# A Fourier filter feeding a gated network: constant third-stage matrix and a reordered first batch

## The chip, the cores and the metric

The kernel runs on one core of one Trainium2 chip. The metric is the device time of one execution in microseconds (us), and a lower time is better. The profile of one execution, taken by the hardware profiler, is read beside it; its span covers the recorded instructions, and the execution's own time is about 2 us longer. The engines are named as the profile names them: PE (matrix products; PEld is its weight load), DVE (vector), ACT (scalar functions), POOL (general purpose), SP (here only an issuer of transfers).

## The reference

```python
def _attn_ref(x, filt_r, filt_i):            # x: 8 x 3136 x 256
    X = np.fft.rfft(x, axis=1)
    F = (filt_r + 1j * filt_i)[None, :, :]
    return np.fft.irfft(X * F, n=x.shape[1], axis=1).astype(np.float32)

def _moe_ref(x, w_in, conv_w, w_out):        # d_ff = 1024
    h = np.maximum(x @ w_in, 0.0)
    ...                                      # conv_out: 3 taps of h along the sequence, a weight per column
    gate = 1.0 / (1.0 + np.exp(-conv_out))
    return (h * gate @ w_out).astype(np.float32)
```

Each batch is filtered in the frequency domain along the sequence, and the filtered sequence goes through the gated network. The weights of the network come as 64-bit floats.

## The kernel before

The sequence of 3136 is split as 112 x 28, and the transform and its inverse are four stages of small matrix products, each done in 14 pieces ("pairs" q, two of 28 columns each). The first stage multiplies by a table `s1` that differs for every column; the second multiplies by one constant matrix `s2`; the filter multiplies the result by the filter's real and imaginary parts (three DVE operations and one POOL add, in `filt`); the third stage multiplies by a table `i1` that differs for every piece; the fourth multiplies by one constant matrix `m2`. The result `y` is kept in SBUF as a rounded part `yh` and a remainder `yl`, since the network's products are made of three products of such parts (`mm3`).

Work stands in two parts of the program.

**The first batch.** No network work can run until batch 0 is through all four stages, so PE has only the transform then. A first loop over q does the first stage into `at`. A second loop over i runs a pipeline: the transposes of pair i (`turn_back`), the second stage of i-1, the third stage of i-4 (`turned_stage`, which puts the pair on the side of the weights and the table on the moving side) into `bt`, and the filter of i-2. After it, four pairs of the first stage of batch 1 (`AHEAD`, by `by_column`) are made and stored to DRAM by transfers that ACT issues. A last loop over q transposes back (`br`), does the fourth stage, and writes `yh` by ACT and `yl` by DVE (`hi_act`, `lo_dve`). Beside it the weights are turned from 64-bit floats into two 32-bit parts: eight chunks, each with seven DVE operations, one POOL add (`to_f32`), two ACT roundings and two POOL subtractions (`split_weights`). A generator hands out these DVE operations a few at a time: `conversion(2)` behind each pair of the first stage, `conversion(1)` behind each i of the second loop, `conversion(2)` behind each pair of the last.

**The stream.** Then a loop over steps m runs the network on units of 510 tokens, eight steps to a unit, with the transform of the next batches in between by a plan: the numbers `at2` and `at4` say at which step of a batch's 48 the second and the fourth stage of a pair stand, and a third stage stands three steps after its second. In this part a third stage is `by_column`, two products of 256 columns with the pair's own table. Units that span two batches are put together in a buffer of their own by `join_tail` and `join_head`, at the steps `tails` and `heads`.

Every engine works through its instructions in the order of the program; the order of transfers on SP is that of the program too. SP's next transfer waits where its buffer is still in use, and all that stands behind it waits as well. The number of buffers is the `bufs` of each tile.

Of the kernel before, what the change touches and what calls it, by code (L numbers as in the profile page):

```python
# [18 lines left out]
N2 = 28  # L19
# [17 lines left out]
def _dft_tables():  # L37
# [7 lines left out]
    n1, n2, c, a = np.arange(N1), np.arange(N2), np.arange(N2), np.arange(N1)  # L45
    s1 = np.zeros((N1, N2, 112))
    m2 = np.zeros((112, N1))
    i1 = np.zeros((2, 2, 28, G, N2, 4))
    for g in range(G):
        for s in range(2):  # L50
            if g == G - 1 and s == 1:
                s1[:, :, 2 * 28 + g] = 1.0
                s1[:, :, 3 * 28 + g] = ((-1.0) ** n1)[:, None]
                m2[2 * 28 + g] = 1.0 / S
                m2[3 * 28 + g] = (-1.0) ** a / S
                i1[0, s, 0, g, :, 2] = 1.0
                i1[1, s, 0, g, :, 2] = (-1.0) ** c
                for j in range(14):
                    if j:
                        w = np.conj(_w(j * c, N2))  # L60
                        i1[0, s, j, g, :, 2] = 2 * w.real
                        i1[1, s, j, g, :, 2] = -2 * w.imag
                    w = np.conj(_w((56 + 112 * j) * c, S))
                    i1[0, s, 14 + j, g, :, 3] = 2 * w.real
                    i1[1, s, 14 + j, g, :, 3] = -2 * w.imag
                continue
# [4 lines left out]
            w = np.conj(_w(k1 * a, N1))  # L71
            m2[2 * s * 28 + g] = 2 * w.real / S
            m2[(2 * s + 1) * 28 + g] = -2 * w.imag / S
            for j in range(28):
                k2, sg = (j, 1) if j < 14 else (41 - j, -1)
                w = np.conj(_w((k1 + 112 * k2) * c, S))
                i1[0, s, j, g, :, 2 * s] = w.real
                i1[1, s, j, g, :, 2 * s] = -sg * w.imag
                i1[0, s, j, g, :, 2 * s + 1] = w.imag
                i1[1, s, j, g, :, 2 * s + 1] = sg * w.real  # L80
# [24 lines left out]
    i1 = i1.reshape(2, 56, G, 112)  # L105
    i1 = np.concatenate([i1[0], np.zeros((8, G, 112)), i1[1]])
    return {"s1": s1, "s2": s2(False), "s2s": s2(True), "one": np.eye(128), "i1": i1, "m2": m2}
# [15 lines left out]
def tile_fft_filter_gated_ffn(  # L123
# [12 lines left out]
    i1: bass.AP,  # L136
    m2: bass.AP,
    out: bass.AP,
# [50 lines left out]
    m2_sb = wc.tile([112, N1], F32, name="m2_sb")  # L189
    s2_sb = wc.tile([112, 120], F32, name="s2_sb")  # L190
    s2s_sb = wc.tile([112, 120], F32, name="s2s_sb")
    one_sb = wc.tile([128, 128], F32, name="one_sb")
# [39 lines left out]

    def second(ps, q, r):
        if q < NP - 1:
            nc.tensor.matmul(ps[0:120], lhsT=s2_sb, rhs=r.rearrange("p j d -> p (j d)"), start=True, stop=True)  # L235
        else:
            for j, m in ((0, s2_sb), (1, s2s_sb)):
                nc.tensor.matmul(ps[0:120, j * D:j * D + D], lhsT=m, rhs=r[:, j], start=True, stop=True)
# [11 lines left out]
    def fourth(ps, br, m=m2_sb):  # L250

        for j in range(2):
            for k in range(KT):
                o = ps[:, (2 * k + j) * N1:(2 * k + j + 1) * N1]
                nc.tensor.matmul(o, lhsT=br[:, j, 128 * k:128 * k + 128], rhs=m, start=True, stop=True)  # L255
# [6 lines left out]
    with (  # L262
# [5 lines left out]
        m2g = sc.tile([112, N1], F32, name="m2g", bufs=1)  # L268
        bt = sc.tile([128, KT, G, 112], F32, name="bt", bufs=1)

        def load_weights(k):
            raws[k] = raw = sc.tile([128, 2, 512], I32, name="raw", bufs=3)
            for part, src in enumerate((w_in, w_out)):
                nc.sync.dma_start(out=raw[:, part], in_=src[:, 512 * k:512 * k + 512])

        def load_conv():
            raws["c"] = raw = sc.tile([128, 2, 512], I32, name="raw", bufs=3)
            nc.sync.dma_start(out=raw[:, 0, 0:6 * NF], in_=conv_w)

        def convert(k):  # L280
# [3 lines left out]
            if k == "c":  # L284
                n = 3 * NF
                yield from to_f32(cw.rearrange("p k f -> p (k f)"), raw[:, 0, 0:2 * n], em[:, 0, 0:n], em[:, 1, 0:n])
            else:
                ws[k] = w = sc.tile([128, 2, 256], F32, name="ws", bufs=4)
                yield from to_f32(w.rearrange("p t n -> p (t n)"), raw.rearrange("p t n -> p (t n)"), em[:, 0], em[:, 1])

        def convert_all():
            for k in range(8):
                yield from convert(k)
                if k + 3 < 8:
                    load_weights(k + 3)
                if k > 0:
                    split_weights(k - 1)
            split_weights(7)

        def split_weights(k):  # L300
            w = ws.pop(k)
            parts = [[t.rearrange("p a b -> p (a b)")[:, 256 * k:256 * k + 256] for t in h] for h in (wi, wo)]
            for part, (wh, wl) in enumerate(parts):
                hi_act(wh, w[:, part])
            for part, (wh, wl) in enumerate(parts):
                lo_pool(wl, w[:, part], wh)
# [29 lines left out]
        with tc.tile_pool(name="sq", bufs=2) as sq:  # L336
            at = sq.tile([128, KT, N2, 112], F32, name="at", bufs=1)

            def table(kind, c):
                k, src, n = {"1": (112, s1, 7), "3": (120, i1, 3)}[kind]  # L340
# [395 lines left out]
```

## Time and profile before

| | before |
|---|---|
| median of 3 runs | 1586.04 us (1582.65 to 1586.32) |
| the profiled execution's own time | 1583.21 us |
| its span | 1581.2 us |
| PE busy | 1532.2 us, 97% of the span |
| DVE, ACT, POOL busy | 75%, 73%, 52% |
| last `yl` of batch 0 begins | 118.06 us |

The table gives shares of the whole span. The first 119 us and the rest have different limits, so the prediction reads them apart, by stretches of time.

### The profile page before, as it was taken

Reading aid. Unit: us, or ns where it says so; the run is one execution under the profiler, and the core shown is the slowest. Engines: PE = TensorE matmul, PEld = TensorE weight load, DVE = VectorE, ACT = ScalarE, POOL = GpSimd, SP = SyncE. Lnnn points to the kernel's source line nnn. Section 1 sums busy time; section 2 is a strip of 40 time slices with the busy share of each in tenths; the row PEclk is TensorE's granted clock in tenths of the full one; section 3 lists DMA queues with packets and bytes.
Section 4 is the critical chain, followed back from the end, with each engine's and each line's share of the span. In section 5 each row is a group of like instructions: output and inputs, shape, how many; then the busy total and the mean of one; then the engine's idle time right before and its main releaser. Section 6 shows DMA issues by size and latency. Waiting matters only on the chain.

```text
span 1581.2 us, 26837 instructions
## 1 busy us (share of the span) xinstructions
PE 1532.2 (97%) x9384; PEld 1334.5 (84%) x9384; DVE 1180.3 (75%) x1810; ACT 1150.4 (73%) x1989; POOL 821.7 (52%) x703
## 2 busy tenths in 40 slices
PE   6879999999999999999999999999999999999999
PEld 5777789878898889988898878987899878989998
DVE  5856876677767877777766787777866887777776
ACT  3367668866687668866688667876678666888886
POOL 2623455544575455744556454754457445664444
PEclk9989999999999999999999999999999999999999
DMA  9808764366634674277543766246742553300000
GB/s 271 261 24 246 226 192 140 119 204 178 186 88 143 201 218 125 74 209 210 155 139 107 212 179 184 85 148 198 211 135 63 179 155 106 96 14 28 27 28 30
DMA packets 160592, 229.16 MB, mean 145 GB/s; under 512 B 16546, under 2 KB 109578, under 8 KB 160458
## 3 DMA queue, kind: packets, MB, share of 16 engines
q1 hardware_dynamic: 159497, 226.53, 48.0%
q8 instruction: 75, 1.23, 0.3%
q10 hardware_dynamic: 960, 0.92, 0.2%
q14 instruction: 60, 0.48, 0.1%
HBM read 156.74 MB, written 70.65 MB: 144 GB/s over the span
## 4 chain that ended last, share of the span: by engine, by line
PE 87%; DMA 3%; issue 3%; ACT 2%; DVE 2%; POOL 1%; SPq 0%; ACTq 0%; POOLq 0%; DVEq 0%
PE ps_h L175 11%; PE ps_h L176 11%; PE ps_h L177 11%; PE po L514 11%; PE po L515 11%; PE po L516 11%; PE ps_t L231 10%; PE ps_t L255 6%; PE ps_t L235 5%; DMA rows<-in_x 1%; DMA f<-in_filt 1%; POOL g L150 1%; DMA tab<-in_i 1%; ACT y L144 0%; ACT br L327 0%
## 5 line engine op out<-in xcount | busy, mean ns | idle before, releaser
L482 DVE SCALAR_TENSOR_TENSOR t<-ps_h,cw,t 128x510 f32<-128x510 f32 (+1 forms) x800 | 588.3, 736 | 308.2 <-ACT t L478 305.0
L150 POOL TENSOR_TENSOR g<-t,g 128x510 fp32r<-128x510 f32 (+1 forms) x400 | 505.8, 1273 | 219.5 <-ACT g L144 203.9
L514 PE MATMUL po<-wo,g 128*128 128x256 f32 (+1 forms) x1576 | 439.3, 279 | 0.2 <-DVE ot L527 0.2
L515 PE MATMUL po<-wo,g 128*128 128x256 f32 (+1 forms) x1576 | 438.3, 278 | 0.0
L516 PE MATMUL po<-wo,g 128*128 128x256 f32 (+1 forms) x1576 | 438.0, 278 | 0.0
L473 ACT ACTIVATE ps_h<-ps_h 128x512 f32<-128x512 f32 (+1 forms) x400 | 234.7, 587 | 242.2 <-PE ps_h L177 240.7
L478 ACT ACTIVATE t<-ps_h,cw 128x510 f32<-128x510 f32 (+1 forms) x400 | 272.7, 682 | 103.4 <-POOL g L150 71.3
L247 POOL TENSOR_TENSOR z<-z,v 120x512 f32<-120x512 f32 x112 | 148.0, 1322 | 383.4 <-DVE v L246 314.6
L175 PE MATMUL ps_h<-y,wi 128*128 128x512 f32 (+1 forms) x688 | 325.3, 473 | 0.0
L514 PEld LDWEIGHTS po<-wo,g 128*128 128x128 f32 (+1 forms) x1576 | 296.6, 188 | 17.8 <-ACT t L478 0.6
L515 PEld LDWEIGHTS po<-wo,g 128*128 128x128 f32 (+1 forms) x1576 | 296.2, 188 | 16.6
L516 PEld LDWEIGHTS po<-wo,g 128*128 128x128 f32 (+1 forms) x1576 | 296.4, 188 | 0.6 <-POOL g L150 0.5
L176 PE MATMUL ps_h<-y,wi 128*128 128x512 f32 (+1 forms) x688 | 269.4, 392 | 0.2 <-DVE y L147 0.2
L488 DVE TENSOR_TENSOR t<-ps_h,t 128x510 f32<-128x510 f32 (+1 forms) x400 | 268.4, 671 | 0.9 <-ACT t L485 0.8
L177 PE MATMUL ps_h<-y,wi 128*128 128x512 f32 (+1 forms) x688 | 269.0, 391 | 0.0
L485 ACT ACTIVATE t<-t 128x510 f32<-128x510 f32 (+1 forms) x400 | 245.2, 613 | 1.8 <-DVE t L482 1.7
L144 ACT ACTIVATE g<-t 128x510 fp32r<-128x510 f32 (+1 forms) x400 | 245.1, 613 | 0.2 <-DVE t L488 0.2
L150 POOL TENSOR_TENSOR y<-z,y 128x448 fp32r<-128x448 f32 x98 | 138.7, 1425 | 97.4 <-ACT y L144 92.9
L175 PEld LDWEIGHTS ps_h<-y,wi 128*128 128x128 f32 x688 | 129.9, 189 | 35.9 <-issue 16.6
L176 PEld LDWEIGHTS ps_h<-y,wi 128*128 128x128 f32 x688 | 130.4, 190 | 34.4 <-issue 16.7
L177 PEld LDWEIGHTS ps_h<-y,wi 128*128 128x128 f32 x688 | 129.6, 188 | 29.8
L226 ACT ACTIVATE st<-ps_t 112x512 f32<-112x512 f32 x192 | 113.2, 591 | 10.9 <-PE ps_t L231 10.9
(81 smaller groups left out, 1657.9 us busy)
## 6 DMA issues: line engine op xcount, KB each, us to landing
filt<-in_filt SPq DMA_DIRECT2D x98, 512.0 KB
tin<-a_dram SPq DMA_DIRECT2D x98, 224.0 KB
b_dram<-st SPq DMA_DIRECT2D x98, 224.0 KB
tin<-b_dram SPq DMA_DIRECT2D x98, 224.0 KB
tin<-in_x SPq DMA_DIRECT2D x94, 224.0 KB
a_dram<-st SPq DMA_DIRECT2D x94, 224.0 KB
out<-ot SPq DMA_DIRECT2D x45, 256.0 KB
tab<-in_i SPq DMA_DIRECT2D x98, 105.0 KB
```

The lines of the kernel that those rows point to most:

```text
L144: nc.scalar.activation(dst, src, AF.Copy)
L150: nc.gpsimd.tensor_tensor(out=dst, in0=src, in1=hi.bitcast(F32), op=ALU.subtract)
L175: nc.tensor.matmul(ps, lhsT=wh, rhs=rh, start=start, stop=False, **kw)
L176: nc.tensor.matmul(ps, lhsT=wh, rhs=rl, start=False, stop=False, **kw)
L177: nc.tensor.matmul(ps, lhsT=wl, rhs=rh, start=False, stop=stop, **kw)
L478: nc.scalar.activation(t, hs[u, f][:, 1:n + 1], AF.Copy, scale=cw[:, 1, f:f + 1])
L482: nc.vector.scalar_tensor_tensor(out=t, in0=h[:, k:place(u)[2] + k], scalar=cw[:, k, f:f + 1], in1=t, op0=ALU.mult, op1=ALU.add)
L485: nc.scalar.activation(ts[u, f], ts[u, f], AF.Sigmoid)
L488: nc.vector.tensor_mul(ts[u, f], hs.pop((u, f))[:, 1:place(u)[2] + 1], ts[u, f])
L514: nc.tensor.matmul(o, lhsT=gh[:, c:c + n], rhs=wo[0][:, f], start=first, stop=False, skip_group_check=True)
L515: nc.tensor.matmul(o, lhsT=gh[:, c:c + n], rhs=wo[1][:, f], start=False, stop=False, skip_group_check=True)
L516: nc.tensor.matmul(o, lhsT=gl[:, c:c + n], rhs=wo[0][:, f], start=False, stop=last, skip_group_check=True)
```

## The change

The third stage's twiddle factors are moved to the fourth stage's tables. With that the third stage's matrix is one constant (`s3`, and `s3s` for the one special column), and the fourth stage has a table for each of its 28 columns (`m2`, and `m2g` with its rows in another order for the first batch). In the stream the third stage becomes one product of 512 columns, and the tables that are loaded are those of the first and the fourth stage. In the first batch the constant matrix is copied once by POOL into `by_r`, in the order in which the third stage reads it; before, each table was read there with a step of four elements.

The weight conversion in the first batch moves: three DVE operations behind each pair of the first stage from q = 2 on, none in the second loop up to i = 14, three behind each of its last three turns, two behind each pair of the last loop. POOL makes the rounding that ACT made. Four chunks of weights are loaded among the first stage's data instead of two, the other four late in the second loop. The filters have five buffers instead of three. The four pairs of batch 1 stand inside the second loop's last turns. In the stream `at4` and `heads` move by one step or two.

```diff
+    def s3(special):
+        m = np.zeros((2, 2, 28, N2, 4))
...
+                w = np.conj(_w(k2 * c, N2))
...
-            w = np.conj(_w(k1 * a, N1))
+            w = np.conj(_w(k1 * n, S))
             m2[2 * s * 28 + g] = 2 * w.real / S
...
+    def by_row(o, q, r, m, ms):
+        if q < NP - 1:
+            nc.tensor.matmul(o, lhsT=m, rhs=r.rearrange("p j d -> p (j d)"), start=True, stop=True)
+        else:
+            for j, t in ((0, m), (1, ms)):
+                nc.tensor.matmul(o[:, j * D:j * D + D], lhsT=t, rhs=r[:, j], start=True, stop=True)
...
+    def third(ps, q, z):
+        by_row(ps[0:112], q, z, s3_sb, s3s_sb)
...
-                nc.tensor.matmul(o, lhsT=br[:, j, 128 * k:128 * k + 128], rhs=m, start=True, stop=True)
+                nc.tensor.matmul(o, lhsT=br[:, j, 128 * k:128 * k + 128], rhs=tab[:, j], start=True, stop=True)
...
             for part, (wh, wl) in enumerate(parts):
-                hi_act(wh, w[:, part])
+                nc.gpsimd.tensor_copy(wh, w[:, part])
...
             def load_filter(q):
-                fts[q] = f = sq.tile([128, 2, 2, D], F32, name="f", bufs=3)
+                fts[q] = f = sq.tile([128, 2, 2, D], F32, name="f", bufs=5)
...
             def load_x(b, q):
-                rows["1", q] = load_in(sq, "1", b, q, 12, "rows")
+                rows["1", q] = load_in(sq, "1", b, q, 8, "rows")
...
-                if c in (1, 3):
-                    load_weights(c // 2)
+                if c in (0, 2, 3, 5):
+                    load_weights((c + 1) // 2)
...
                 nc.scalar.activation(at[:, :, pair(q)], ps, AF.Copy)
-                conversion(2)
+                if q >= 2:
+                    conversion(3 if q < 12 else 2)
+            for t, s in zip(by_r, (s3_sb, s3s_sb)):
+                nc.gpsimd.tensor_copy(t, s.rearrange("p (c r) -> p r c", r=4))
...
+                if 0 <= i - NP < AHEAD:
+                    ps = bank()
+                    by_column(ps, tab("1", i - NP), rows.pop(("1", i - NP)))
+                    store(tp, "1", 1, i - NP, ps, 3, "st", nc.scalar)
                 if 0 <= i - 4 < NP:
                     q = i - 4
-                    ps = turned_stage(zs.pop(q), [tab("3", q)[:, j].rearrange("p (c r) -> p r c", r=4) for j in range(2)])
+                    ps = turned_stage(zs.pop(q), [by_r[q == NP - 1 and j].rearrange("p r c -> p (r c)") for j in range(2)])
...
-                conversion(1)
+                if i in (7, 9, 11, 13):
+                    load_weights(4 + (i - 7) // 2)
...
+                if i == 12:
+                    for c in range(3):
+                        table("4", c)
+                if i >= NP + 1:
+                    conversion(3)
...
-            ot = wp.tile([128, 2, D], F32, name="ot", bufs=3)
+            ot = wp.tile([128, 2, D], F32, name="ot", bufs=2)
...
-            at2, at4 = [8 + 3 * q // 2 for q in range(NP)], [33 + 11 * q // NP for q in range(NP)]
+            at2, at4 = [8 + 3 * q // 2 for q in range(NP)], [35 + 10 * q // NP for q in range(NP)]
...
-            at2, at4 = [2 + 9 * q // 5 for q in range(NP)], [32 + 12 * q // NP for q in range(NP)]
+            at2, at4 = [2 + 9 * q // 5 for q in range(NP)], [33 + 12 * q // NP for q in range(NP)]
...
-        tails[w + 29] = heads[w + 45] = next(u for u in range(NU) if joins(u) and place(u)[0] == t - 1)
+        tails[w + 29] = heads[w + 46] = next(u for u in range(NU) if joins(u) and place(u)[0] == t - 1)
...
-            k, src = {"1": (112, s1), "3": (120, i1)}[op[0]]
-            got_table[op] = t = tp.tile([120, 2, 112], F32, name="tab", bufs=4)[0:k]
+            src = {"1": s1, "4": m2}[op[0]]
+            got_table[op] = t = tp.tile([112, 2, 112], F32, name="tab", bufs=4)
...
-            by_column(ps, w, got_z.pop((b, q)))
+            third(ps, q, got_z.pop((b, q)))
...
-    nc = bacc.Bacc("TRN2", target_bir_lowering=False, num_devices=1, dynamic_dma_scratch_size=8192)
+    nc = bacc.Bacc("TRN2", target_bir_lowering=False, num_devices=1, dynamic_dma_scratch_size=1024)
```

Three places in the order of instructions show it. Each row is a line of the program, the operation, what it writes and reads, and the size. `ps` is a PSUM bank, `f` a filter, `z` and `v` the filter's results, `em`, `raw` and `ws` belong to the weight conversion.

SP, behind the loads of the first stage. Before:

```order
L221 DMA tin<-in_x 112x512 x3
L274 DMA raw<-in_w_in 128x512
L274 DMA raw<-in_w_out 128x512
L342 DMA tab_313<-in_i 120x448
L342 DMA tab_315<-in_i 120x448
L349 DMA f<-in_filt 128x1024 x3
L342 DMA tab_323<-in_i 120x448
L377 DMA m_sb<-in_m 112x112
L379 DMA m2g<-in_m 28x112 x4
```

After:

```order
L291 DMA raw<-in_w_in 128x512
L291 DMA raw<-in_w_out 128x512
L351 DMA tab_221<-in_s 112x448
L232 DMA rows<-in_x 112x512 x2
L358 DMA f<-in_filt 128x1024 x7
L232 DMA tin<-in_x 112x512
L358 DMA f<-in_filt 128x1024 x2
L232 DMA tin<-in_x 112x512
L358 DMA f<-in_filt 128x1024 x2
```

The filters now stand right behind the last pair of the first stage; the stream's first inputs (`tin`) and the weights stand behind or among them.

DVE, at the first filters. Before:

```order
L160 TENSOR_SCALAR em<-raw 128x512
L244 TENSOR_TENSOR z<-ps,f 120x512
L245 TENSOR_TENSOR v_87<-ps,f 56x512
L246 SCALAR_TENSOR_TENSOR v_87<-ps,f 56x512
L162 TENSOR_TENSOR em<-em 128x512
L244 TENSOR_TENSOR z<-ps,f 120x512
L245 TENSOR_TENSOR v_88<-ps,f 56x512
L246 SCALAR_TENSOR_TENSOR v_88<-ps,f 56x512
L164 TENSOR_SCALAR em<-raw 128x512
```

After:

```order
L178 TENSOR_SCALAR em<-ws 128x512
L261 TENSOR_TENSOR z<-ps,f 120x512
L262 TENSOR_TENSOR v_88<-ps,f 56x512
L263 SCALAR_TENSOR_TENSOR v_88<-ps,f 56x512
L261 TENSOR_TENSOR z<-ps,f 120x512
L262 TENSOR_TENSOR v_89<-ps,f 56x512
L263 SCALAR_TENSOR_TENSOR v_89<-ps,f 56x512
```

The fourteen filters now follow each other without an operation of the conversion between them.

DVE, in the last loop, where `y_755` and `y_728` are the remainder `yl`. Before:

```order
L162 TENSOR_TENSOR em<-em 128x512
L147 TENSOR_TENSOR y_755<-ps,y_754 128x2x2x112
L164 TENSOR_SCALAR em<-raw 128x512
L166 SCALAR_TENSOR_TENSOR ws<-em 128x512
L147 TENSOR_TENSOR y_755<-ps,y_754 128x2x2x112
L168 TENSOR_SCALAR em<-ws 128x512
L170 SCALAR_TENSOR_TENSOR em<-raw,em 128x512
L147 TENSOR_TENSOR y_755<-ps,y_754 128x2x2x112 x12
```

After:

```order
L172 TENSOR_TENSOR em<-em 128x512
L157 TENSOR_TENSOR y_728<-ps,y_727 128x2x2x112
L174 TENSOR_SCALAR em<-raw 128x512
L176 SCALAR_TENSOR_TENSOR ws<-em 128x512
L157 TENSOR_TENSOR y_728<-ps,y_727 128x2x2x112
L178 TENSOR_SCALAR em<-ws 128x512
L180 SCALAR_TENSOR_TENSOR em<-raw,em 128x512
L157 TENSOR_TENSOR y_728<-ps,y_727 128x2x2x112
L168 TENSOR_SCALAR em<-raw 128x512
L170 TENSOR_SCALAR em<-raw 128x512
L157 TENSOR_TENSOR y_728<-ps,y_727 128x2x2x112
```

Before, two pairs of conversion operations stand among the 14 remainders; now nine pairs do, up to the tenth remainder, and eleven operations stand between the last filter and the first remainder.

More of the change, by code (lines that the diff above doesn't have):

```diff
@@ L135, in tile_fft_filter_gated_ffn @@
     one: bass.AP,
-    i1: bass.AP,
+    s3: bass.AP,
+    s3s: bass.AP,
     m2: bass.AP,
+    m2g: bass.AP,
     out: bass.AP,
@@ L248, in filt, with fourth @@
         return z
-    def fourth(ps, br, m=m2_sb):
+    def fourth(ps, br, tab):
         for j in range(2):
@@ L267, in tile_fft_filter_gated_ffn, with convert_conv @@
         raws, ws, fts, tabs, rows, zs, pss = {}, {}, {}, {}, {}, {}, {}
-        m2g = sc.tile([112, N1], F32, name="m2g", bufs=1)
+        by_r = [sc.tile([120, 4, N2], F32, name=f"by_r{i}", bufs=1) for i in range(2)]
         bt = sc.tile([128, KT, G, 112], F32, name="bt", bufs=1)
         def load_weights(k):
[L272 to L278, printed above, removed]
+            raws[k] = raw = sc.tile([128, 2, 512], I32, name="raw", bufs=4)
+            for part, w in enumerate((w_in, w_out)):
+                nc.sync.dma_start(out=raw[:, part], in_=w[:, 512 * k:512 * k + 512])
+        def convert_conv():
+            n = 3 * NF
+            em = sc.tile([128, 2, 512], I32, name="em")
+            yield from to_f32(cw.rearrange("p k f -> p (k f)"), conv_raw, em[:, 0, 0:n], em[:, 1, 0:n])
         def convert(k):
@@ L283, in convert, with convert_all @@
             em = sc.tile([128, 2, 512], I32, name="em")
[L284 to L301, printed above, removed]
+            w = sc.tile([128, 2, 256], F32, name="ws", bufs=2)
+            yield from to_f32(w.rearrange("p t n -> p (t n)"), raw.rearrange("p t n -> p (t n)"), em[:, 0], em[:, 1])
             parts = [[t.rearrange("p a b -> p (a b)")[:, 256 * k:256 * k + 256] for t in h] for h in (wi, wo)]
             for part, (wh, wl) in enumerate(parts):
-                hi_act(wh, w[:, part])
+                nc.gpsimd.tensor_copy(wh, w[:, part])
             for part, (wh, wl) in enumerate(parts):
                 lo_pool(wl, w[:, part], wh)
+        def convert_all():
+            yield from convert(0)
+            yield from convert_conv()
+            for k in range(1, 8):
+                yield from convert(k)
         def bank():
@@ L337, in tile_fft_filter_gated_ffn @@
             at = sq.tile([128, KT, N2, 112], F32, name="at", bufs=1)
+            conv_raw = sq.tile([128, 6 * NF], I32, name="conv_raw", bufs=1)
             def table(kind, c):
[L340 to L341 removed]
+                pool, src, n = {"1": (sq, s1, 4), "4": (sc, m2g, 3)}[kind]
+                tabs[kind, c] = t = pool.tile([112, 4, 112], F32, name=f"tab{kind}", bufs=n)
                 nc.sync.dma_start(out=t, in_=src[:, 4 * c:4 * c + 4])
@@ L412, in tile_fft_filter_gated_ffn @@
                 ps = bank()
-                fourth(ps, rows.pop(("4", q - 1)), m2g)
+                fourth(ps, rows.pop(("4", q - 1)), tab("4", q - 1))
+                if q % 2 == 0 and q // 2 + 2 < 7:
+                    table("4", q // 2 + 2)
                 yh, yl = y_slices(0, pair(q - 1))
@@ L580, in tile_fft_filter_gated_ffn @@
     inputs = [op for _, op in order if op[0] in "124"]
-    tables = [op for _, op in order if op[0] in "13"]
+    tables = [op for _, op in order if op[0] in "14"]
     filters = [op for _, op in order if op[0] == "2"]
```

99 lines of the change are left out of this document (46 added, 53 removed).

## The prediction

> **What bounds the kernel now.** I read the busy shares by stretches first (stretch; length, busy time and instructions of PE, PEld, DVE, ACT, POOL; clock, DMA share, GB/s):
>
> ```profile
> 0.00:28.00 28.00, 18.01 (x112) 17.41 (x112) 9.83 (x24) 10.25 (x20) 5.42 (x12) 0.88 0.97 263
> 28.00:38.00 10.00, 6.41 (x28) 3.69 (x28) 9.65 (x14) 3.56 (x8) 5.09 (x5) 1.00 0.90 273
> 38.00:79.00 41.00, 34.64 (x159) 29.01 (x160) 36.54 (x56) 12.71 (x25) 25.45 (x20) 0.93 0.90 266
> 79.00:93.00 14.00, 8.28 (x36) 6.80 (x35) 7.30 (x9) 4.25 (x9) 5.03 (x5) 0.73 0.19 55
> 93.00:119.10 26.10, 23.68 (x169) 22.61 (x169) 16.10 (x18) 21.37 (x34) 5.72 (x19) 0.87 0.03 8
> 119.10:1581.20 1462.10, 1441.21 (x8881) 1255.02 (x8881) 1100.83 (x1691) 1098.25 (x1896) 775.01 (x645) 1.00 0.47 142
> ```
>
> The last row is the stream: PE is busy 98.6% of it, 20.9 us are idle, so there only PE work counts. The rows above are the first batch: 119.1 us with 28.1 us of idle PE, transfers near their limit up to 79 us and nearly none behind it. Its ends are in the rows of the timeline (start, length): the last copy of stage 1, the first second-stage product, the first and the last filter operation, the first `yl`,
>
> ```profile
> 27.53 0.54 ACT L370 ACTIVATE at<-ps 128x448 f32<-128x448 f32 x1 [0.35 <-PE ps L317]
> 29.51 1.12 PE L235 MATMUL ps<-ar,s_sb 112*120 112x512 f32 x2 [0.25 <-ACT ar L327]
> 38.05 0.69 DVE L244 TENSOR_TENSOR z<-ps,f 120x512 f32<-120x512 f32 x1
> 78.07 0.69 DVE L246 SCALAR_TENSOR_TENSOR v<-ps,f 56x512 f32<-56x512 f32 x1
> 96.58 0.98 DVE L147 TENSOR_TENSOR y<-ps,y 128x448 fp32r<-128x448 f32 x1 [10.00 <-ACT y L144]
> ```
>
> and in the chain that ended last, from the last third stage on:
>
> ```profile
> 82.42 2.05 PE ps L317 x8
> 84.47 1.72 PE ps L231 x4
> 86.21 0.61 ACT st L226
> 86.84 4.32 DMA a_dram<-st
> 91.24 0.61 ACT st L226
> 91.87 0.31 ACTq L227
> 92.55 0.40 ACT wo L144
> 92.95 0.49 ACT br L327
> 93.48 2.05 PE ps L255 x8
> ...
> 118.06 1.00 DVE y L147
> 119.20 0.47 PE ps_h L176
> ```
>
> The back transform has its columns at 84 us, but ACT stands behind the fourth store (its buffer waits 4.3 us for a transfer) and behind two weight roundings, so the first fourth-stage product begins at 93.48. The stream's first product waits for the last `yl`. So the time is the length of the first batch plus a full PE, and I price the change as four lengths before 119.1 and one behind.
>
> **A, up to the first filter (38.1 us before).** Transfers per issue, in KB:
>
> ```profile
> f<-in_filt SPq DMA_DIRECT2D x14, 512.0 KB
> rows<-in_x SPq DMA_DIRECT2D x18, 224.0 KB
> raw<-in_w_in SPq DMA_DIRECT2D x8, 256.0 KB
> tab<-in_s SPq DMA_DIRECT2D x7, 196.0 KB
> ```
>
> `raw` comes in pairs, so a chunk of weights is 512 KB; `tin` has the size of `rows`. Before, four chunks, three `tin` and two `i1` tables stand between stage 1 and the first filter. After, nothing does: 14 x 224 + 7 x 196 + 4 x 512 and some 300 KB of constants are 6854 KB, 7.02 MB. At 263 GB/s they take 26.7 us. Two chunks more than before stand ahead of the last `rows` (1.05 MB, 4.0 us), but before PE was behind its data there (six pairs back to back at the end), so I let stage 1 end 2.4 us later, at 30.4 us. From there the chain of transposes, copy and first second-stage product was 28.07 to 30.63, 2.6 us. A is 33.1 us: 5.0 us gained. Bounds: 31 (no delay) and 35 (the whole 4.0 us).
>
> **B, the fourteen filters (40.7 us before).** Before, a turn is bound by PE: its work in a stretch of the filters, in a stretch of the back transform, and by tile (ns min/median/max), with the second stage in the chain:
>
> ```profile
> 47.50:70.50 23.00, 23.00 (x112) 18.91 (x111) 20.32 (x32) 9.32 (x18) 14.79 (x11) 1.00 0.96 279
> 104.45:115.10 10.65, 10.65 (x98) 10.65 (x98) 8.11 (x8) 10.65 (x17) 0.88 (x3) 1.00 0.01 2
> L317 PE MATMUL ps<-tab,rows x112: 274/275/527, 4.4 to 27.2; 112*128 112x112 f32 x112
> L317 PE MATMUL ps<-tab,z x112: 362/382/556, 42.0 to 84.1; 120*128 120x112 f32 x112
> 144.58 0.86 PE ps_t L235 x2
> ```
>
> A turn is 14 instructions, so 2.88 us at full clock. A pair of the back transform is 12 (four transposes, eight products with 112 columns read without a step): 1.30 us. With 0.86 us for the second stage a turn with eight such products would be 2.16 us, so a third stage that reads `by_r` saves 0.7 us; the same product takes 275 ns from a plain table and 382 ns from the one read with a step. [...]
>
> DVE's share of a turn and what else stands in it (instructions on the filters `f`, on the conversion's `em`, then one of them by ns min/median/max, then groups):
>
> ```profile
> 38.00:79.00 41.00, 28.97 (x42) 0.93 0.90 266
> 8.00:105.00 97.00, 35.42 (x56) 10.51 (x8) 0.86 0.73 209
> L160 DVE TENSOR_SCALAR em<-raw x9: 170/453/1495, 6.0 to 84.4; 128x512 int32<-128x512 int32 x8, 128x24 int32<-128x24 int32 x1
> L247 POOL TENSOR_TENSOR z<-z,v 120x512 f32<-120x512 f32 x14 | 21.6, 1547 | 15.5 <-DVE v L246 14.4 <-PE ps L325 1.2
> L147 DVE TENSOR_TENSOR y<-ps,y 128x448 fp32r<-128x448 f32 x14 | 14.1, 1004 | 16.3 <-ACT y L144 16.3
> ```
>
> Three filter operations are 42 in 28.97 us, 2.07 a turn; a conversion operation is 35.42 / 56 = 0.63 us, and one a turn goes away. POOL's 1.55 is hidden below both. By PE the last filter ends at 33.1 + 13 x 2.16 + 2.1 = 63.3 us. By transfers: ahead of the last filter's arrival stand 14 filters, two `tin`, two chunks, two `s1` tables and four `rows`, 9928 KB or 10.17 MB, at 279 GB/s 36.5 us; from 26.7 they end at 63.2, and with 1 us to land and the filter itself at 66.3. The five buffers let SP issue four turns ahead, so its waits for a buffer cost nothing while a filter lands within 8 us. I take 65: B is 31.9 us, 8.8 gained. Bounds 63 and 73 (PE as slow as now: 33.1 + 13 x 2.88 + 2.1).
>
> **C, from the last filter to the first `yl` (78.8 to 96.6, 17.8 us).** DVE now has eleven conversion operations there, 6.9 us. Beside them: POOL's add 1.5, third stage 0.9, copy 0.5, transposes 1.0, copy 0.6, fourth stage 1.0, `yh` 1.0, 6.5 us. The four pairs of batch 1 now stand in the turns before; their first store comes some 5 us before ACT needs its buffer again, against 4.3 us of transfer in the quiet, so 0 to 3 us remain of that wait; I take 1. The roundings are off ACT. On POOL they cost what casts of this kind do, between these sizes,
>
> ```profile
> L453 POOL CAST yx<-y x14: 242/572/959, 232.8 to 1337.3; 128x156 fp32r<-128x156 f32 x2, 128x310 fp32r<-128x310 f32 x2, 128x464 fp32r<-128x464 f32 x2, 128x618 fp32r<-128x618 f32 x2
> ```
>
> so about 0.4 us for 256 columns: a chunk on POOL is 1.3 + 0.8 + 1.5 = 3.6 us, and nobody in the first batch waits for it but the next chunk's buffers, 7 us later. C is 8.0 us, 9.8 gained; bounds 7 and 12.
>
> **D, fourteen `yl` (96.6 to 119.1, 22.5 us).** PE and ACT can go at 1.30 us a pair, but DVE has 14 x 1.00 + 18 x 0.63 = 25.4 us in front of the last one: 2.9 us lost. DVE becomes the bound here. Bounds 22 (every operation at L160's median, 0.45) and 30 (0.9, half way to its longest and a little less). The seven `m2g` tables (196 KB each, in place of seven `i1` and five small ones) are loaded where transfers are idle.
>
> **E, the stream.** A third stage of 512 columns takes what two of 256 take (0.86 us, four records or two), the fourth's shape is unchanged, and as many tables are loaded as before, 98 KB for 105, later in each batch, where transfers are rare. Later `at4` and `heads` eat one step, 1462.1 / 400 = 3.7 us, of the time between the joining copy and its first product, 294.6 to 305.7 us:
>
> ```profile
> L459 ACT ACTIVATE yx<-y x7: 298/675/1017, 294.6 to 1396.1; 128x868 fp32r<-128x868 f32 x1, 128x714 fp32r<-128x714 f32 x1, 128x560 fp32r<-128x560 f32 x1, 128x406 fp32r<-128x406 f32 x1
> L175 PE MATMUL ps_h<-yx,wi x112: 388/397/800, 305.7 to 1447.6; 128*128 128x512 f32 x112
> ```
>
> POOL's copy ends 2 us behind ACT's, so some 5 us stay. Two output buffers for three: each is used again a unit (29 us) later, hidden. [...] I take 1 us gained, between 6 gained (a third of the idle) and 5 lost.
>
> **Sum.** The stream starts at 33.1 + 31.9 + 8.0 + 25.4 = 98.4 instead of 119.1: 20.7 us, and 21.7 with E. From the profiled execution's 1583.2 us that is 1561.5. The median shown is 2.8 us above that execution; I set 1563 for the median.
>
> **Rivals.** (1) The filters stay at PE's or the transfers' old pace: B ends at 73, time 1571. For it: 0.96 of DMA busy already, and rates of 263 where small transfers mix in. Against: the two rows of the same product. [...] (2) Fewer tables where the second and third stages crowd the queue free some of the stream's 20.9 us: 1557. For it: the tables move to where the fourth stage stands, without `i1` beside the filters. Against: PE is 98.6% busy, and as many tables come as before. (3) POOL's casts and adds hold up DVE's conversion: steps of 1.49 us occur beside POOL's adds (the row of L160 above), and if each of the 29 in C and D took that, 25 us more make 1588, slower than before; it decides from a mean of 1.38 us on. Against: the mean was 0.63 with POOL busy 62% of the filters' time. [...] (4) Nothing gained: the tightened chain waits elsewhere, for example `yh` for the first batch's buffers, as long as it did: 1585.
>
> **Chances.** The forecast 0.64 (1556 to 1568), (1) 0.16, (2) 0.12, (3) 0.03, (4) 0.05. The range 1553 to 1574 holds the first three with their bounds. About 0.3%, 5 us, is what can be told from no change: faster 0.93, same 0.04, slower 0.03.
>
> **What would show it.** A: first filter at 33. B: 2.1 to 2.3 us a filter, the product from `by_r` at 275 ns. C: no DMA of `a_dram` in the chain. D: nine `yl` 2.2 us apart, DVE in the chain, stream from 98. E: PE busy as before in the last 1462 us. A filter end behind 70, or a stream that lasts over 1467 us, makes the forecast wrong.

## The result, and the profile after

The changed kernel took 1562.05 us in the median of four runs (1560.39 to 1566.38), the kernel before 1586.11 (1582.65 to 1586.32). The medians differ by 24 us. The ratio is 0.986, with a 95% interval of 0.983 to 0.988, which is 22.5 us, 19 to 26. The forecast was 1563. The profiled execution took 1562.33 us, its span is 1560.5.

So the sum held; its terms did not hold as well. The stretches of the changed kernel (columns as in the prediction):

```profile
0.00:28.00 28.00, 17.73 (x92) 16.94 (x93) 15.79 (x28) 7.36 (x13) 10.96 (x20) 0.93 0.89 237
28.00:38.00 10.00, 7.78 (x37) 6.46 (x37) 4.38 (x7) 2.93 (x7) 2.87 (x6) 0.69 0.84 303
37.45:70.48 33.03, 30.80 (x194) 23.94 (x193) 28.97 (x42) 15.12 (x28) 16.54 (x13) 1.00 0.87 271
70.48:80.70 10.22, 8.21 (x66) 7.38 (x65) 9.95 (x13) 6.69 (x11) 8.82 (x9) 1.00 1.00 295
80.70:104.83 24.13, 17.14 (x124) 15.04 (x123) 23.75 (x32) 15.95 (x22) 13.91 (x30) 0.95 0.09 27
104.83:1560.50 1455.67, 1440.55 (x8703) 1224.00 (x8701) 1101.48 (x1692) 1098.07 (x1896) 774.08 (x645) 1.00 0.47 142
```

Rows three to five are B, C and D, and the last row is the stream. The third number of busy time is DVE's, in B, C and D 28.97, 9.95 and 23.75 us of 33.03, 10.22 and 24.13. From the first filter to the last `yl` DVE is busy for 62.7 of 67.4 us. Before the change the first batch waited for PE, for transfers and for ACT; now nearly all of it behind the first filter is DVE's.

The marks of the timeline (start, length), to be set against those in the prediction, and the end of the chain:

```profile
34.31 0.54 ACT L384 ACTIVATE at<-ps 128x448 f32<-128x448 f32 x1 [1.15 <-PE ps L325]
36.29 1.12 PE L246 MATMUL ps<-ar,s_sb 112*120 112x512 f32 x2 [0.25 <-ACT ar L335]
37.45 0.69 DVE L261 TENSOR_TENSOR z<-ps,f 120x512 f32<-120x512 f32 x1 [4.30 <-PE ps L246]
65.64 0.69 DVE L261 TENSOR_TENSOR z<-ps,f 120x512 f32<-120x512 f32 x1 [2.33 <-DMA f<-in_filt]
69.79 0.69 DVE L263 SCALAR_TENSOR_TENSOR v<-ps,f 56x512 f32<-56x512 f32 x1
80.70 1.02 DVE L157 TENSOR_TENSOR y<-ps,y 128x448 fp32r<-128x448 f32 x1
```

```profile
73.08 4.91 DMA tab<-in_s
78.01 0.43 DVE em L168
78.45 1.43 DVE em L170
...
79.90 0.77 DVE em L172
...
80.70 1.02 DVE y L157
...
96.07 0.94 DVE y L157
97.00 0.34 DVE em L174
...
97.44 1.03 DVE ws L176
98.47 0.91 DVE y L157
```

No transfer of `a_dram` and no rounding is left in this chain: from 78 us on, `yl` and conversion operations alternate on DVE. The chain reaches 78.01 by a transfer of 4.9 us, but DVE was idle for only 0.27 us of C, so that transfer cost next to nothing. The last `yl` ends at 104.8 (119.1 before).

| stretch | before | forecast | after |
|---|---|---|---|
| A, up to the first filter | 38.1 | 33.1 | 37.45 |
| B, fourteen filters | 40.7 | 31.9 | 33.0 |
| C, to the first `yl` | 17.8 | 8.0 | 10.2 |
| D, fourteen `yl` | 22.5 | 25.4 | 24.1 |
| stream, from the last `yl` | 1462.1 | 1461.1 | 1455.7 |

The first batch became 14.2 us shorter and not 20.7; the stream 6.4 us shorter and not 1. Two errors, of 6.5 and 5.4 us, nearly cancelled.

### The profile page after: what moved, and what is told of

Its sections match the earlier page's. It is cut to its first block, busy times and chain, and to the rows that moved or that the text cites. A ratio compares the mean times of both kernels' runs of the same rounds, so it can differ in the third digit from the quotient of the medians.

```text
span 1560.5 us, 26465 instructions
## 1 busy us (share of the span) xinstructions
PE 1521.7 (98%) x9202; PEld 1293.3 (83%) x9202; DVE 1183.8 (76%) x1810; ACT 1146.0 (73%) x1973; POOL 827.2 (53%) x721
## 4 chain that ended last, share of the span: by engine, by line
PE 91%; DVE 3%; DMA 3%; issue 1%; ACT 1%; SPq 0%; POOL 0%; ACTq 0%; DVEq 0%; POOLq 0%
PE ps_h L185 12%; PE ps_h L186 12%; PE ps_h L187 12%; PE po L532 12%; PE po L533 11%; PE po L534 11%; PE ps_t L246 10%; PE ps_t L272 6%; PE ps_t L242 5%; DMA raw<-in_w_out 1%; DMA rows<-in_x 1%; PE ps_t L249 1%; DVE y L157 1%; DMA tab<-in_s 1%; DVE v L262 1%
## 5 line engine op out<-in xcount | busy, mean ns | idle before, releaser
L264 POOL TENSOR_TENSOR z<-z,v 120x512 f32<-120x512 f32 x112 | 144.5, 1290 | 387.5 <-DVE v L263 306.7
L185 PEld LDWEIGHTS ps_h<-y,wi 128*128 128x128 f32 x688 | 130.0, 189 | 43.2 <-issue 22.5
L186 PEld LDWEIGHTS ps_h<-y,wi 128*128 128x128 f32 x688 | 130.3, 189 | 41.1 <-issue 24.1
L187 PEld LDWEIGHTS ps_h<-y,wi 128*128 128x128 f32 x688 | 129.6, 188 | 29.6
```

The costliest lines, as they stand in the source:

```text
L185: nc.tensor.matmul(ps, lhsT=wh, rhs=rh, start=start, stop=False, **kw)
L186: nc.tensor.matmul(ps, lhsT=wh, rhs=rl, start=False, stop=False, **kw)
L187: nc.tensor.matmul(ps, lhsT=wl, rhs=rh, start=False, stop=stop, **kw)
```

## The experiments

All times below are medians; where runs were made on different chips, I compare ratios to the kernel before on the same chip. One caution on marks within a single execution: five runs with the same first stage (the changed kernel and four of the kernels below) had their first filter at 35.8, 36.8, 37.45, 37.6 and 37.9, so a mark carries about a microsecond either way.

**The step in the third stage's matrix.**

```diff
-ps = turned_stage(zs.pop(q), [by_r[q == NP - 1 and j].rearrange("p r c -> p (r c)") for j in range(2)])
+ps = turned_stage(zs.pop(q), [(s3s_sb if q == NP - 1 and j else s3_sb).rearrange("p (c r) -> p r c", r=4) for j in range(2)])
```

> The changed kernel with the third stage of the first batch reading the constant matrix in a step of four numbers, as the tables were read before, and not from the copy that is laid out in order. Theory: the product of 112 columns goes back from 275 to about 382 ns, a turn of the filter loop from 2.17 to 2.6 to 2.9 us on TensorE, the fourteen filters take 6 to 9 us longer (39 to 42 from 33.0), the time is 1567 to 1571. [...]

1567.33 us, ratio 0.9886 (0.9872 to 0.9900), against 1562.67 and 0.9858 (0.9844 to 0.9872) for a kernel of the same set whose first batch is the changed one. The third-stage product by tile, first of the changed kernel, then of this one, and who made DVE wait beside the filters of this one:

```profile
L325 PE MATMUL ps<-by_r,z x112: 259/275/363, 41.1 to 73.3; 120*128 120x112 f32 x112
```

```profile
L325 PE MATMUL ps<-s_sb,z x108: 362/378/388, 41.9 to 79.5; 120*128 120x112 f32 x108
```

```profile
DVE z L261 <- PE ps L325: 8.0, 10, 1.2
DVE z L261 <- PE ps L246: 6.1, 1, 6.1
```

The same data, the same shape, only the order of the elements read: 275 against 378 ns. The filters wait for PE in ten turns, their stretch is 37.8 us and not 33.0 (4.8 us longer; 6 to 9 were expected), and the last `yl` ends 5.0 us later, at 109.8. What the forecast said of the step is shown.

**The same step taken out of the kernel before.**

```diff
+i1r = i1.reshape(120, G, N2, 4).transpose(0, 1, 3, 2).reshape(120, G, 112)
...
-k, src, n = {"1": (112, s1, 7), "3": (120, i1, 3)}[kind]
+k, src, n = {"1": (112, s1, 7), "3": (120, i1r, 3)}[kind]
...
-ps = turned_stage(zs.pop(q), [tab("3", q)[:, j].rearrange("p (c r) -> p r c", r=4) for j in range(2)])
+ps = turned_stage(zs.pop(q), [tab("3", q)[:, j] for j in range(2)])
```

The edit gives the first batch a table of its own, `i1r`; the later batches still read `i1`, other than the expectation says.

> The kernel before with its third stage's tables laid out in the order in which the first batch reads them, so that its product reads without a step, and nothing else changed (the later batches then read them in another order, which changes the numbers of the output but not the work). Theory, that its turn of 2.88 us is TensorE's, and VectorE with its conversion operation needs about 2.7: 14 times 0.18, 2 to 4 us faster, 1581 to 1583. Rival, that the whole of what the step cost in the changed kernel (about 5 us) comes off here too: 1579.5 to 1581. Second rival, that the table transfers set the pace: no change, 1584 to 1586.

1584.38 us, ratio 0.9990 (0.9976 to 1.0004): no change that can be told. The products did get shorter (a median of 275 ns for 382), and DVE waited for something else (waits of DVE from 38 to 80 us, of SP from 20 to 82 us, then the products by shape, busy time and mean ns):

```profile
DVE z L246 <- DMA f<-in_filt: 5.8, 5, 3.0
```

```profile
SPq L351 <- DVE v L248: 13.9, 10, 2.2
```

```profile
L319 PE MATMUL ps<-tab,z 120*128 120x112 f32 x90 | 13.7, 298 | 11.7 <-POOL z L249 11.6
```

The kernel before shows 0.8 us of DVE's wait, and 7.6 us in six turns of SP's, which is a filter's load waiting until DVE frees a buffer. There the filters stood on two limits of nearly the same height, PE and the arrival of `f`; taking one away shows the other. The second rival's number holds, no change; that it is the tables' bytes is what the next run tests. The step was worth 5 us only in the kernel whose transfers had been rearranged.

**The tables' transfers put back beside the filters.**

```diff
+def spare(c):
+    t = sq.tile([112, 4, 112], F32, name="spare", bufs=3)
+    nc.sync.dma_start(out=t, in_=s1[:, 4 * c:4 * c + 4])
+for c in range(3):
+    spare(c)
...
+if q % 2 and q // 2 + 3 < 7:
+    spare(q // 2 + 3)
```

> The changed kernel with seven table transfers of 196 KB put back beside the filters at the places where the kernel before had its third stage's tables; nothing reads them. Theory, that the filters of the kernel before were held by transfers nearly as much as by TensorE, so that the constant matrix pays through the bytes it saves too: last filter 3 to 6 us later than 70.5 (1.4 MB at 279 GB/s are 5 us), 1564 to 1568. Rival, that five filter buffers hide the transfers: last filter within 1.5 us, 1561 to 1563.5.

1565.44 us, ratio 0.9873 (0.9854 to 0.9892). The last filter ended at 71.6 and the last `yl` at 105.9, each 1.1 us later, and the filters' stretch is 34.8 us for 33.0; the waits for `f` rose, from the first to the second of these rows:

```profile
DVE z L261 <- DMA f<-in_filt: 2.9, 2, 2.3
```

```profile
DVE z L261 <- DMA f<-in_filt: 4.3, 2, 3.3
```

The marks are the rival's, the median lies in the theory's range, and the interval overlaps that of the changed kernel. So the bytes of the tables are a small term, of 1 to 3 us; that the other limit of the last run lay in the depth of the filter buffers (three, now five) or in the order of the loads is likely, since SP waited there for a buffer in ten turns, and was not tried apart.

**Conversion put back among the filters.**

```diff
-if i >= NP + 1:
-    conversion(3)
+if i >= 2:
+    conversion(1)
...
-if i in (7, 9, 11, 13):
-    load_weights(4 + (i - 7) // 2)
+if i in (0, 3, 6, 9):
+    load_weights(4 + i // 3)
```

> The changed kernel with conversion put back among the filters: one conversion operation in each of the last sixteen turns of the filter loop, where there was none before turn 15, and the last four pieces of the weights loaded 3 to 7 turns earlier for it. All work is still done. Theory, that the change of the loop is that VectorE is the bound from the first filter to the last yl and a conversion costs its 0.6 to 0.9 us wherever it stands: filters 6 to 9 us longer, the stretches behind them 6 to 9 us shorter, 1560 to 1565. Rival, that taking the conversion out of the filter loop was itself the gain: 1568 to 1572.

1560.47 us, ratio 0.9838 (0.9821 to 0.9855): not slower, if anything 2 us faster. B, C and D of this kernel:

```profile
36.48:75.63 39.15, 34.19 (x192) 25.04 (x191) 37.85 (x55) 15.12 (x27) 26.70 (x23) 0.93 0.85 259
75.63:82.66 7.03, 5.58 (x42) 4.71 (x42) 4.58 (x7) 3.81 (x7) 5.62 (x10) 1.00 0.58 161
82.66:102.06 19.40, 18.50 (x151) 17.26 (x149) 19.26 (x25) 17.95 (x26) 7.97 (x18) 1.00 0.15 42
```

The filters take 6.1 us longer, C and D 7.9 us less, and DVE is busy 61.7 of 65.6 us. The diff's most visible edit, no conversion among the filters, is worth nothing by itself: DVE is the bound of the whole stretch, and an operation cost about the same in both places: in this run 0.68 us in the mean for the 13 among the filters and 0.73 for the 16 behind them (single ones 0.41 to 1.64), against 0.76 for the 29 behind them in the changed kernel.

**Rounding on ScalarE again.**

```diff
-nc.gpsimd.tensor_copy(wh, w[:, part])
+hi_act(wh, w[:, part])
```

> The changed kernel with the rounding of the weights on ScalarE again, as in the kernel before, and not on POOL. Theory, that POOL's roundings lengthen VectorE's conversion operations (0.90 us each behind the last filter, 0.45 alone) but VectorE has other work behind them: stretch behind the last filter 1 to 3 us shorter than 10.2, the last yl 0 to 2 us earlier, 1559 to 1562. Rival, that ScalarE is short between the filters and the yl units: ACT's copies come late, 1563 to 1566.

1576.41 us, ratio 0.9934 (0.9916 to 0.9952), 12 us slower than the changed kernel. Both expectations were too small. The filters end where they did (70.55), the first `yl` is 3.2 us later and the last 11.6 us, at 116.4. The waits between 70 and 105 us:

```profile
ACT wi L154 <- POOL ws L182: 15.2, 4, 7.1
POOL ws L182 <- DVE em L180: 14.3, 3, 6.7
PEld ps L272 <- ACT br L335: 9.2, 3, 5.0
DVE y L157 <- ACT y L154: 8.9, 5, 3.4
```

Together they are a ring: ACT stands before a rounding until POOL has added, POOL until DVE has converted, and meanwhile `br` and `yh`, queued behind the rounding on ACT, hold up PE and so DVE's `yl`. None of ACT's operations here is long (between 84 and 116 us of this run a rounding took 0.4 us, `br` 0.61, `yh` 1.0); the order of one queue makes them expensive. On POOL the rounding waits as well (in the changed kernel POOL waited 10.6 us for DVE from 70 to 105 us, in four turns), but nothing on the way to the end stands behind it.

**Rounding on POOL alone, in the kernel before** (the same edit the other way round).

> The kernel before with the rounding of the weights on POOL, nothing else changed. Theory, that the 12 us which ScalarE's rounding cost in the changed kernel came only because the conversion stood beside the yl units there; in the kernel before two or three roundings stand behind the last filter, 0.4 us each on ScalarE's path: 0 to 4 us faster, 1582 to 1586. Rival, that the rounding on POOL is the main term of the change by itself: 8 to 12 us faster, 1575 to 1579.

1581.28 us, ratio 0.9969 (0.9957 to 0.9980): 5 us faster (3 to 7), a little more than the theory's 0 to 4 and far from the rival's 8 to 12. D became 4.1 us shorter (18.4 us for 22.5), and the last `yl` came 2.6 us earlier, since the filters of this execution took 2.3 us longer (43.0 for 40.7; the run with the new due times, whose first batch is that of the kernel before, has 43.1). So ACT's rounding costs 12 us only where conversion stands beside the `yl`; moving conversion there without moving the rounding would have lost about half of what the change gained.

**The due times of the yl units and the heads, both ways.**

```diff
-at2, at4 = [8 + 3 * q // 2 for q in range(NP)], [35 + 10 * q // NP for q in range(NP)]
+at2, at4 = [8 + 3 * q // 2 for q in range(NP)], [33 + 11 * q // NP for q in range(NP)]
...
-at2, at4 = [2 + 9 * q // 5 for q in range(NP)], [33 + 12 * q // NP for q in range(NP)]
+at2, at4 = [2 + 9 * q // 5 for q in range(NP)], [32 + 12 * q // NP for q in range(NP)]
...
-tails[w + 29] = heads[w + 46] = next(u for u in range(NU) if joins(u) and place(u)[0] == t - 1)
+tails[w + 29] = heads[w + 45] = next(u for u in range(NU) if joins(u) and place(u)[0] == t - 1)
```

The other run makes the opposite edit in the kernel before. The two expectations name the numbers the wrong way round; the edit is the one shown here: 35, 33 and 46 are the new times, 33, 32 and 45 the old ones.

> The changed kernel with the old due times of the yl units and of the stream's heads (35 + 10q/14, 33 + 12q/14, w + 46 in place of 33 + 11q/14, 32 + 12q/14, w + 45). The first batch is left as changed, so its last yl should stand at 104.8 again. Theory, that the 5 to 7 us which the stream gained over my -1 come from the moved due times: about 1567 (1562.1 + 5), with the waits of TensorE in the stream back near 17 us from 11.8. Rival, that they come from the shorter first batch and the fewer tables that are loaded and read in it: 1561 to 1563, and the stream from the last yl stays at 1455.7.

> The kernel before with the new due times of the yl units and of the stream's heads alone (33 + 11q/14, 32 + 12q/14, w + 45). Theory, that the due times are worth about 5 us whatever the first batch does: 1579 to 1582, with the waits of TensorE in the stream down from 17 to about 12 us. Rival, that they suit only the earlier stream of the changed kernel: 1584 to 1588.

The changed kernel with the old times: 1567.13 us, 0.9888 (0.9872 to 0.9904), against 0.9858. The kernel before with the new times: 1583.34 us, 0.9978 (0.9964 to 0.9993). Where it lies is read from one row each, the first and the last product of a joined unit (one that spans two batches); before (in the prediction) it is 305.7 to 1447.6. After, after with old times, before with new times:

```profile
L185 PE MATMUL ps_h<-yx,wi x112: 388/397/800, 292.1 to 1426.9; 128*128 128x512 f32 x112
```

```profile
L185 PE MATMUL ps_h<-yx,wi x112: 388/397/800, 291.1 to 1430.2; 128*128 128x512 f32 x112
```

```profile
L175 PE MATMUL ps_h<-yx,wi x112: 388/397/800, 310.0 to 1448.4; 128*128 128x512 f32 x112
```

The lengths are 1141.9 before, 1134.8 after, 1139.1 and 1138.4: between these products the new due times save 4.3 us in the one kernel and 3.5 in the other. But 1.6 us of that is spent ahead of the first of them: from the last `yl` to it are 187.3 us after and 185.7 with the old times, 186.6 before and 188.2 with the new. Of the whole stream, from the last `yl` on, 2.7 us (1458.4 to 1455.7) and 1.9 us (1462.1 to 1460.2) remain. The sum of TensorE's waits from 120 us on agrees: 12.4 to 10.9 us and 17.4 to 15.6. By the ratios of the runs the due times are worth 4.8 and 3.5 us, with intervals of 2 to 3 us either way. So the theory has the direction in both kernels, and its 5 us is at the upper end (the time of the second run lies between its two ranges).

**The length of the third stage's product in the later batches.**

```diff
-by_row(ps[0:112], q, z, s3_sb, s3s_sb)
+for j in range(2):
+    m = s3s_sb if q == NP - 1 and j else s3_sb
+    nc.tensor.matmul(ps[0:112, j * D:j * D + D], lhsT=m, rhs=z[:, j], start=True, stop=True)
```

> The changed kernel, but the seven later batches make the third stage as two products of 256 columns with the constant matrix, as the kernel before did with its tables, and not as one of 512 columns with a correction for the last pair. 98 products of 512 become 196 of 256. Theory, that the stream's gain in the batches 2 to 7 (about 1.2 us each) comes from the longer product: some 7 us back, 1566 to 1569. Rival, that it comes from the table loads left out or the plan: within 1.5 us of 1562.1.

1562.67 us, ratio 0.9858 (0.9844 to 0.9872), the changed kernel's. The same length between joined units is 1136.2, 1.4 us more than after. The theory falls; two products of 256 columns cost what one of 512 does, within 1.4 us in the 91 pairs in which the kernels differ (the last pair of each batch is two products in both).

**How many weights ahead of the first filter: all eight pieces, a fifth one, only three.** The first is made from the changed kernel, the others from the one with conversion among the filters, whose first filter stands at 36.5; their edits are shown against it.

```diff
-if c in (0, 2, 3, 5):
-    load_weights((c + 1) // 2)
+load_weights(c)
...
+    load_weights(7)
...
-if q >= 2:
-    conversion(3 if q < 12 else 2)
+conversion(6)
...
-if i in (7, 9, 11, 13):
-    load_weights(4 + (i - 7) // 2)
```

> The changed kernel with all eight pieces of the weights loaded and converted in the first stage (six conversion operations per pair there, none behind the filters). Loads of 2 MB more stand before the first filter. Theory, that VectorE is the bound from the first filter to the last yl: the stretch behind the last filter and the yl units lose about 18 operations at 0.67 us, while the first stage, which waits for transfers, grows by 3 to 8 us: 1553 to 1560. Rival, that the transfers bound all of the first 60 us: the first filter is 8 us later or more, and what is saved behind it only pays it back: 1562 to 1568.

1574.81 us, ratio 0.9927 (0.9908 to 0.9945). C and D are 25.8 us (34.3 after), as the theory said, but the first filter is at 55.2: 18 us lost, and 4.5 more in the filters, for 8.5 saved. A wait of SP and one of DVE before the first filter, the stretch ahead of it, and the end of that stretch on DVE:

```profile
SPq L291 <- DVE em L180: 2.2, 1, 2.2
```

```profile
DVE em L168 <- DMA raw<-in_w_out: 9.1, 1, 9.1
```

```profile
28.00:55.00 27.00, 16.39 (x60) 12.11 (x60) 25.80 (x33) 5.27 (x10) 21.66 (x24) 0.91 0.59 198
```

```profile
54.58 0.69 DVE L180 SCALAR_TENSOR_TENSOR em<-raw,em 128x512 f32<-128x512 uint32 x1
55.19 0.68 DVE L261 TENSOR_TENSOR z<-ps,f 120x512 f32<-120x512 f32 x1
```

The issue of a late piece waits for a buffer, DVE then for its data, and the filters stand behind its conversion on DVE, which goes on to the last microsecond before the first filter. The time lies beyond both expectations. The late first filter is the rival's, but by the order of DVE's queue and not by the rate of the transfers: their share is only 0.59 there.

```diff
+if c == 6:
+    load_weights(4)
...
-conversion(3 if q < 12 else 2)
+conversion(4 if q < 7 else 3)
...
-if i in (0, 3, 6, 9):
-    load_weights(4 + i // 3)
+if i in (0, 3, 6):
+    load_weights(5 + i // 3)
```

> The changed kernel with conversion among the filters (as in the run with one operation a turn), and a fifth piece of the weights loaded and mostly converted in the first stage, where VectorE is idle almost half of the time. Theory, that VectorE is the bound from the first filter on: seven operations of 0.6 to 0.7 us leave it, 4 to 5 us, and the piece delays the first filter by 2 us (512 KB at 237 GB/s): 1 to 3 us faster than the run it is made from, 1557.5 to 1559.5. Rival, that the fifth piece holds up the rows' transfers as all eight did: first filter 4 us later or more, 1561 to 1566.

1560.65 us, ratio 0.9837 (0.9815 to 0.9860), the same as the run it is made from. The first filter stands 1.2 us later, within what such a mark varies by, and the last `yl` ends 2.6 us later, at 104.7. Neither expectation holds. DVE's wait behind the filters shows where its saving went:

```profile
DVE y L157 <- ACT y L154: 6.9, 11, 3.8
```

In the run that it is made from this wait is 2.3 us, once. Here DVE is ready in eleven turns before ACT's `yh` is, and PE is busy for 19.00 of the 19.31 us of D (18.50 of 19.40 there). With fewer conversion operations on DVE, the back transform on PE and ACT sets the pace of the `yl`.

```diff
-if c in (0, 2, 3, 5):
+if c in (0, 2, 3):
     load_weights((c + 1) // 2)
...
-conversion(3 if q < 12 else 2)
+conversion(3 if q < 6 else 2)
...
-if i in (0, 3, 6, 9):
-    load_weights(4 + i // 3)
+if i in (0, 3, 6, 9, 12):
+    load_weights(3 + i // 3)
```

> The changed kernel with conversion among the filters, and the fourth piece of the weights loaded behind the first stage's rows and not ahead of them, its conversion behind too. Theory, that the first filter came 4.4 us later than I forecast because the weights' bytes stand ahead of the last rows: first filter 2 us earlier than 36.5, and since six operations move behind it, the time 0 to 3 us longer than the run it is made from. Rival, that the rate of the transfers or the engines set the end of the first stage: first filter within 0.7 us of 36.5, and the time 3 to 5 us longer.

1565.31 us, ratio 0.9869 (0.9851 to 0.9888), 5 us longer than its parent. Its first filter is the earliest of all:

```profile
34.74 0.69 DVE L261 TENSOR_TENSOR z<-ps,f 120x512 f32<-120x512 f32 x1 [8.95 <-PE ps L246]
```

1.7 us before its parent's, and 1.1 us before the earliest with four pieces ahead: the weights' bytes do stand in the way, by about the time that 512 KB take (2.2 us at 237 GB/s, an estimate). But six conversion operations now follow the filters' start, and the whole is slower: the mark is the theory's, the price the rival's. The last `yl` ends at 104.5 against 102.1; the other half of the price lies behind the first batch and stays unexplained.

The two fastest, with conversion among the filters and four or five pieces of the weights ahead of them, cannot be told from the changed kernel by their intervals.

## Why the prediction was right

The time was met partly by luck. The first batch was forecast 6.4 us too short (A by 4.4, C by 2.2, B by 1.1, D 1.3 too long), the stream 5.4 us too long, and no run shows that the one error caused the other. Had the stream given only its 1 us, the time would have been about 1567.5, still inside the range.

**A failed as a size.** 33.1 forecast, 37.45 measured, 0.6 us gained and not 5.0. The term takes 263 GB/s; the rate was 237 in the first 28 us, and at 7.02 MB that is 29.6 us and not 26.7. I let stage 1 end 2.4 us behind the old one, of a bound of 4; its last copy came 6.8 us later (34.31 for 27.53). The run with one piece less ahead confirms the direction, 1.7 us a piece, with a microsecond either way. Most of the rest is PE's pace on the rows that came last. The first two pairs of stage 1, two that began at 22.42, two behind the last wait, and the stretches around the first and the last of these:

```profile
4.42 3.72 PE L325 MATMUL ps<-tab,rows 112*128 112x112 f32 x16 [4.42 <-DMA rows<-in_x]
22.42 2.40 PE L325 MATMUL ps<-tab,rows 112*128 112x112 f32 x16 [2.69 <-DMA rows<-in_x]
30.57 3.71 PE L325 MATMUL ps<-tab,rows 112*128 112x112 f32 x16 [1.34 <-DMA rows<-in_x]
4.00:8.00 4.00, 3.58 (x16) 3.49 (x16) 0.00 (x0) 0.54 (x1) 0.00 (x0) 1.00 0.90 261
24.00:34.00 10.00, 7.98 (x36) 7.50 (x35) 6.05 (x10) 2.29 (x5) 5.00 (x8) 0.50 0.97 323
```

The last two pairs took 1.3 us more than the two at 22.42, and the granted clock was 0.50 from 24 to 34 us. That the clock made the difference is not shown: the first two pairs took as long, 3.72 us, at a granted clock of 1.00. The kernel before had a stretch at 0.50 too, from 20 to 24 us, before the end of its stage 1. I had counted the transfers and not PE's pace behind the last of them.

**B was right in size and incomplete in reason.** 33.0 for 31.9, filters 2.17 us apart (2.16 forecast), the product at 275 ns. Putting the step back costs 4.8 us of the filters and 5 of the time. The end was the transfers', as the second of my two sums for B had it: twelve filters went 2.17 us apart, and the last two waited 2.9 us for `f` (2.3 of it in the row at 65.64). No run shows the 1 us to land that this sum has; the last `f` landed 7.44 us after its issue (60.82 to 68.26). And I priced the 8.8 us as PE's; the kernel before without the step shows that the arrival of `f` alone would have kept the old pace. The five buffers and the new order of the loads, which I used only as a bound, were probably the condition; neither was tried alone.

**C was mis-sized by one number.** Its structure is as forecast: no store in the way, and DVE with eleven conversion operations as its length. They took 9.95 us and not 6.9 (the operations on `em` there and beside the `yl`):

```profile
70.50:80.70 10.20, 9.95 (x11) 2.85 (x2) 1.00 1.00 295
80.70:102.20 21.50, 12.01 (x18) 3.97 (x3) 1.00 0.10 30
```

0.90 us each in C, 0.67 in D: the prediction's 0.63 is a mean over 8 to 105 us of the kernel before, in which POOL was busy for 44.52 of 97 us, against 8.82 of 10.2 and 11.81 of 21.5 in the two rows here. Single steps show what rival 3 spoke of, first on DVE, then what POOL did beside the two long ones:

```profile
71.12 1.49 DVE L168 TENSOR_SCALAR em<-raw 128x512 int32<-128x512 int32 x1
72.53 1.49 DVE L170 TENSOR_SCALAR em<-raw 128x512 int32<-128x512 int32 x1
...
78.01 0.43 DVE L168 TENSOR_SCALAR em<-raw 128x512 int32<-128x512 int32 x1
```

```profile
70.65 1.68 POOL L264 TENSOR_TENSOR z<-z,v 120x512 f32<-120x512 f32 x1 [1.46 <-DVE v L263]
72.29 1.45 POOL L182 TENSOR_TENSOR ws<-ws,em 128x512 f32<-128x512 f32 x1
```

The operation of line 168 took 1.49 us beside an add of POOL, and 0.43 us at 78.01, where it began before POOL's next add (78.17). Over all 29 the mean is 0.76, so the rival was there at about a seventh of its price at most (3.7 us of 25 or more, over my 0.63).

**D was right**: 24.1 for 25.4, DVE in the chain, `yl` about 2.2 us apart at the start. What the prediction wrote off in half a sentence, that the rounding leaves ACT, is what made this length possible: with ACT's rounding D is 32.6 us long. I had priced that edit at its durations, 0.4 us a rounding, and not at the wait of what is queued behind it.

**E failed as a size, to the good.** 6.4 us for 1, just beyond my bound of 6. Seven of the kernels above have the same stream, and in them it took 1456.5 to 1459.8 us from the last `yl` on, so 6.4 is the lucky end and about 5 the fair size. PE is busy as long as before (1440.6 us for 1441.2); what went is idle time, 15.1 us for 20.9. The due times give 1.9 to 2.7 us of that, the longer product 1.7 at most (1457.4 us without it). Some 2 us stay: they would be the constant matrix in place of loaded tables and the other edits of the later batches, rival 2's mechanism; no run took these apart. I had priced the due times only at the one joining copy that they bring closer to its product, and not at the order which they give to PE's work in every batch.

Rival 1 is out by B's marks and rival 4 by the time; of rival 2 the idle time did shrink, but its cause, fewer tables in the way, is not shown.

## What to carry to other kernels

Before pricing an edit, add up the bounding engine over the whole stretch it could move to: here 63 of 67 us were DVE's, and whether its conversion stood among the filters or behind them made no difference, while the small edit beside it (0.4 us operations taken off ACT's queue, where they waited for another engine) was worth 12 us, and 5 in the kernel before. An edit on one of two equal limits shows nothing until the other has gone too, so the same edit can be worth 0 in one kernel and 5 us in the other. And take a duration from where the operation will stand, with the neighbours that it will have, not from a mean over the run.

## What the hardware showed that was not expected

The third stage's product of 112 columns took 378 ns in the median where it read its matrix in a step of four numbers (16 bytes), and 275 ns where it read the same numbers in order. A conversion operation that took 0.43 us at 78.01 took 1.49 us at 71.12, beside an add of POOL, and so did the next one, at 72.53; in the mean the eleven of C took 0.90 us, 0.27 more than the 0.63 of the kernel before, and not the 1.06 more of these two steps. And PE's granted clock was 0.50 from 24 to 34 us, behind a stretch (20 to 24 us) in which PE was busy for 1.58 of 4 us and waited for `rows` up to 22.42; no run shows that the one caused the other.
